# Another instruction order for the engines of a fused attention and two-layer MLP kernel

## The chip, the cores and the metric

The program runs on one core of one Trainium2 chip. The metric is the device time of one execution in microseconds. Three timed runs of the kernel before took 627.49, 627.61 and 626.53 us, a median of 627.49 us. The engines are TensorE (PE in the rows, with PEld for its weight loads), VectorE (DVE), ScalarE (ACT), GpSimd (POOL) and SyncE (SP), whose queue issues nearly all DMAs.

## The reference

```
q_pool = mean of each two neighbouring rows of q          # q, k, v: 2 x 8 heads x 1152 x 64
scores = q_pool @ k^T / 8 ; minus the row's maximum
attn   = exp(scores) / (sum(exp(scores)) + 1e-9)
x      = attn @ v, heads side by side                     # 1152 tokens x 512
x      = g(x @ w_in) @ w_out,  g = h * tanh(softplus(h))  # 512 -> 2048 -> 512
out    = e(x @ w_in2) @ w_out2, e = elu(h)                # 512 -> 2048 -> 512
```

All data is float32.

## The kernel before

The attention works on eight pairs of heads, numbered n = 0 to 7 (batch n // 4). A pair has 576 pooled queries, cut into c = 0 (256) and c = 1 (320), and 1152 keys in nine tiles of 128, numbered kt. Every operand of a score is split into a high and a low part, and three products are added: high with high, low with high, high with low.

The steps of a pair have two-letter names, and the whole attention is one string of such steps, ORDER, which a loop at the end carries out from left to right. Each engine receives its own instructions in that sequence and works them off in that sequence; an instruction whose operands or whose buffer are not ready holds up all that stand behind it on its engine. The names that matter here, each followed by digits for the pair n and then for the piece:

- PM (line 286, also 293, 300, 303) multiplies queries and keys once, for the row maximum alone; PK (line 310, also 312, 314, 318) reduces that product on DVE. TP (lines 324, 327) makes the negated maximum of the pieces.
- FL and FC turn the maximum of pair 0 round through TensorE (line 334) and ACT (lines 341, 345). For the other pairs TO and TI send it through DRAM.
- QK (line 380) is the three products of one tile of scores for c and kt, and a last product (line 387) with "unit" subtracts the maximum. With c = 0 two key tiles are joined in one step. EX (line 398) is the exponential on ACT.
- The sum over the keys has three ways, given for each n and c by a string of nine digits in SUMS, one digit a key tile: 1 adds the tile to a running sum (AD, line 410, on POOL or DVE by its last digit), 2 leaves it to one reduction over neighbouring tiles on DVE (GA, line 415), 0 gives the tile directly to the product with ones on TensorE (SU, line 426). SU also takes the running sum and GA's result: each of these is one source of SU.
- AV (line 471) is the product with v. EV, SP, SO, SI, IN, IO, II, SC, TH, TL bring the sums through DRAM and scale the output.
- LQ, LK, LV load q, k and v; PQ pools q; HQ, DQ (lines 245, 248) and HK, DK (lines 257, 260) split q and k; BQ (line 252) places the last 64 queries. There is one buffer for raw q and one for raw k.
- WR reads a piece of the weights through a ring of three raw buffers. WB (line 119, ACT), WC (line 123, POOL), WS and WW (lines 128, 133, 134, DVE) and WH, WL (lines 142, 145) bring it into its form. A raw buffer is free once WW has read it.

PSUM has four slots of two banks in the attention. The last digit of PM, QK, FL and AV is the slot, so such a step waits until the slot's last reader (PK, EX, FC or EV) is done.

The start of pair 0 stands before ORDER as a few lines of code. The string REST holds the last steps, done between the first units of the MLPs. The MLPs are a fixed sequence of 96 units in bands of 384 tokens, with TensorE products in lines 178 and 709.

Of the kernel before, what the change touches and what calls it, by code (L numbers as in the profile page):

```python
# [22 lines left out]
def tile_pool_attention_mish_elu_mlp(  # L23
# [16 lines left out]
    nc = tc.nc  # L40
# [28 lines left out]
    XH = const.tile([P, KM, NT], F32R, name="XH")  # L69
# [88 lines left out]
    for layer in range(2):  # L158
        c0 = 0
# [23 lines left out]
    def attention():  # L183
        with ExitStack() as st:
# [321 lines left out]
            def ahead_of(i):  # L506
# [26 lines left out]
            LV11 PK07 PQ10 PM083 EX000 PM0c0 PK08 AD0000 AD0030 BQ1 PM091 PK0c HQ1 PM0d2 HK10 PK09 PM0a3 DK100 WB0  # L533
            PK0d PM100 PK0a PM141 QK0062 PK14 WC0 QK0043 EX006 DK110 TP01 PK10 FL11 EX004 DQ10 LK20 PM162 PM120 FC1
            PK16 LQ21 QK0153 LQ20 QK0161 PK12 LK21 EX015 QK0112 EX016 QK0173 AD0051 EX011 QK0130 WS0 EX017 WW0 QK0121
            EX013 PM112 QK0103 EX012 PQ20 PK11 WR30 PM170 EX010 QK0141 WR31 PK17 QK0183 AD0040 EX014 PM132 EX018 PM191
            PK13 PM150 AD0161 AD0130 WH0 QK0083 EX008 TP10 AV00209 PK19 TO10 HQ2 AD0150 HK21 PK15 HK20 TI10 GA00 DK200
            PM263 DK211 EV00 DQ20 PM221 PK26 SU00 LK30 LK31 PM1802 PK22 SP00 WL00 BQ2 SO00 QK1003 PK18 WB1 QK1041 WC1
            SI00 TP11 PM250 TO11 WS1 AV01209 LQ30 WW1 LQ31 TI11 GA01 WH1 WL10 WR40 WB2 PK25 EX100 WC2 IN00 SU01 PQ31
            LV21 EX104 LV20 WS2 EV01 WW2 AD1051 AD1000 QK1110 SP01 BQ3 SO01 PM203 EX111 PM211 IO00 QK1152 PK20 WH2  # L540
            QK1020 EX115 AD1040 PK21 QK1163 EX102 II00 PM242 AD1011 QK1131 EX116 AD1020 PK24 QK1080 SI01 EX113 WR50
            QK1123 EX108 PM231 AD1030 QK1182 EX112 PK23 PM270 EX118 QK1063 WL20 TP20 PK27 TO20 QK1142 EX106 QK1101
            IN01 IO01 PM290 WB3 GA10 AV10309 WC3 WS3 II01 SC00 TH00 EX114 TL00 TI20 WW3 EX110 AD1180 AD1140 SU10 PK29
            PM2823 WR60 WH3 EV10 QK1171 SP10 PK28 SO10 WL30 AV11007 TP21 SC01 TO21 GA11 TH01 HQ3 HK31 DQ30 TI21 EX117
            HK30 TL01 AV11079 DK311 LQ40 LQ41 DK301 PM392 EV11 PM333 PM361 LK41 PK33 SU11 LV30 LK40 PK39 QK2133 SP11
            SO11 PK36 QK2112 EX213 WR41 PM340 EX211 SI10 PM323 PK34 QK2121 PQ40 QK2022 EX212 PK32 PM310 AD2110 AD2120
            QK2041 EX202 PK31 SI11 PM303 QK2002 WR51 EX204 PK30 LV31 PM370 QK2151 AD2041 AD2020 EX200 TP30 QK2183 IN10
            TO30 EX215 IO10 QK2102 AD2011 AD2030 WR61 EX218 QK2161 PK37 EX210 QK2143 EX216 QK2082 AD2101 AD2050 EX214
            PM350 QK2171 IN11 IO11 WB4 GA21 QK2063 EX208 WC4 BQ4 AV20206 EX217 AD2080 EX206 II11 PK35 HK40 AD2060 TI30
            HQ4 DK401 AV20269 II10 HK41 DK411 PM461 DQ41 PM493 LK51 SU20 LK50 PK49 LQ51 PM3802 SP20 LQ50 PK46 SO20  # L550
            AV21309 PK38 TP31 SC10 TO31 SC11 TH10 TH11 TL10 TL11 EV20 TI31 WS4 PQ50 WW4 SU21 EV21 LV40 QK3081 SP21
# [295 lines left out]
```

## Time and profile before

| what | value |
|---|---|
| median of three timed runs | 627.49 us |
| the profiled execution's own time | 623.83 us |
| its span | 621.8 us |
| TensorE busy | 605.3 us, 97% of the span |
| DVE, ACT, POOL busy | 460.5, 338.3, 193.4 us |
| mean granted TensorE clock | 0.992 |
| attention, by the trace | to about 218 us |

The page cuts the span into 40 slices of 15.5 us; the row PEclk is the clock that TensorE was granted in each slice in tenths of full speed, 9 being full (0.9 or more). A busy TensorE is not one at its peak: at half the clock a matmul is busy for twice as long.

### The profile page before, as it was taken

What the parts mean: (1) busy time and instruction counts of PE and PEld (TensorE: products, weight loads), DVE (VectorE), ACT (ScalarE), POOL (GpSimd) and SP (SyncE); (2) the same over time, 40 slices, a digit from 0 to 9 for tenths busy, and PEclk for the clock granted to TensorE, in tenths of its full rate; (3) what the DMA queues carried; (4) which work ended last, traced back from release to release, by engine and by line L of the source; (5) the groups of instructions that cost most, each with busy time, mean ns of one, the idle gap of its engine ahead of it and who ended that gap; (6) DMA issues with size and microseconds to landing.
All of it is one profiled execution on the core that took longest, in us unless ns stands there. A gap on an engine that the chain in (4) does not pass through costs nothing.

```text
span 621.8 us, 11257 instructions
## 1 busy us (share of the span) xinstructions
PE 605.3 (97%) x4434; PEld 534.4 (86%) x4434; DVE 460.5 (74%) x687; ACT 338.3 (54%) x659; POOL 193.4 (31%) x190
## 2 busy tenths in 40 slices
PE   5889999999999999999999999999999999999997
PEld 3757587686786799999999999999999999999996
DVE  5799999899785676754656667669878788995453
ACT  4637485674673464434444453466657666664442
POOL 5665363566965421111132323232210101100000
PEclk9789999999999999999999999999999999999999
DMA  7624243242232035323224222322232123400011
GB/s 213 193 73 122 74 134 106 76 124 70 60 95 57 17 94 164 104 67 101 72 66 135 69 69 67 103 69 70 67 102 69 67 69 106 123 9 17 36 51 51
DMA packets 46958, 53.32 MB, mean 86 GB/s; under 512 B 13818, under 2 KB 36410, under 8 KB 46906
## 3 DMA queue, kind: packets, MB, share of 16 engines
q1 hardware_dynamic: 46762, 52.42, 28.0%
q8 instruction: 34, 0.56, 0.4%
q10 hardware_dynamic: 144, 0.20, 0.1%
q14 instruction: 18, 0.15, 0.1%
HBM read 50.14 MB, written 2.47 MB: 85 GB/s over the span
## 4 chain that ended last, share of the span: by engine, by line
PE 86%; DVE 4%; issue 3%; POOL 3%; ACT 2%; DMA 0%; POOLq 0%; DVEq 0%; ACTq 0%
PE banks L709 32%; PE banks L178 31%; PE banks L471 9%; PE banks L380 7%; PE banks L286 2%; PE banks L387 2%; ACT pt L398 2%; PE banks L426 2%; POOL add L410 1%; DVE stat L310 1%; PE banks L300 1%; DVE wf L133 1%; DVE add L410 1%; PE banks L293 0%; DMA kr<-in_k_dram 0%
## 5 line engine op out<-in xcount | busy, mean ns | idle before, releaser
L178 PE MATMUL banks<-XH,wh 128*128 128x384 f32 x384 | 129.5, 337 | 0.0
L178 PE MATMUL banks<-XL,wh 128*128 128x384 f32 x384 | 129.4, 337 | 0.0
L178 PE MATMUL banks<-XH,wl 128*128 128x384 f32 x384 | 129.4, 337 | 0.0
L123 POOL TENSOR_SCALAR wf<-wf 128x512 f32<-128x512 f32 x64 | 43.3, 678 | 252.2 <-ACT wf L119 214.0
L398 ACT ACTIVATE pt<-banks 128x640 f32<-128x640 f32 (+2 forms) x112 | 82.0, 801 | 17.2 <-PE banks L387 15.4
L310 DVE TENSOR_REDUCE stat<-banks 128x2 f32<-128x1024 f32 (+1 forms) x68 | 77.1, 1167 | 8.8 <-PE banks L286 6.2
L471 PE MATMUL banks<-pt,vr 128*64 128x320 f32 (+1 forms) x576 | 74.1, 411 | 0.8 <-DVE stat L310 0.8
L178 PEld LDWEIGHTS banks<-XH,wh 128*128 128x128 f32 x384 | 72.0, 187 | 2.1 <-issue 0.3
L178 PEld LDWEIGHTS banks<-XL,wh 128*128 128x128 f32 x384 | 72.0, 188 | 1.8
L178 PEld LDWEIGHTS banks<-XH,wl 128*128 128x128 f32 x384 | 72.0, 188 | 0.0
L471 PEld LDWEIGHTS banks<-pt,vr 128*64 128x64 f32 x576 | 40.3, 138 | 30.6 <-issue 2.0
L410 POOL TENSOR_TENSOR add<-add,pt 128x512 f32<-128x512 f32 (+1 forms) x43 | 62.4, 1459 | 8.2 <-DVE add L410 4.3
L709 PE MATMUL banks<-gl,wh 128*128 128x384 f32 x192 | 64.6, 336 | 0.1
L709 PE MATMUL banks<-gh,wl 128*128 128x384 f32 x192 | 64.5, 336 | 0.0
L709 PE MATMUL banks<-gh,wh 128*128 128x384 f32 x192 | 64.4, 335 | 0.0
L663 ACT ACTIVATE gh<-banks 128x384 fp32r<-128x384 f32 x48 | 23.6, 492 | 71.7 <-PE banks L178 71.7
L709 PE MATMUL banks<-wl,gh 128*128 128x512 f32 x144 | 56.2, 390 | 0.0
L709 PE MATMUL banks<-wh,gl 128*128 128x512 f32 x144 | 56.2, 390 | 0.0
L709 PE MATMUL banks<-wh,gh 128*128 128x512 f32 x144 | 56.2, 390 | 0.0
L666 DVE TENSOR_TENSOR gl<-g,gh 128x384 fp32r<-128x384 f32 x48 | 30.6, 640 | 31.1 <-ACT g L664 31.1
L689 ACT CAST gh<-g 128x384 fp32r<-128x384 f32 x48 | 24.7, 514 | 48.1 <-DVE g L683 47.8
L133 DVE SCALAR_TENSOR_TENSOR wf<-raw,wf 128x512 int32<-128x512 int32 x64 | 48.6, 759 | 2.1
(92 smaller groups left out, 1216.5 us busy)
## 6 DMA issues: line engine op xcount, KB each, us to landing
raw<-in_moe_w_in_dram SPq DMA_DIRECT2D x28, 512.0 KB
raw<-in_moe_w_out_dram SPq DMA_DIRECT2D x28, 512.0 KB
vr<-in_v_dram SPq DMA_DIRECT2D x16, 288.0 KB
qr<-in_q_dram SPq DMA_DIRECT2D x14, 288.0 KB
kr<-in_k_dram SPq DMA_DIRECT2D x7, 384.0 KB
out_dram<-part SPq DMA_DIRECT2D x9, 256.0 KB
raw<-in_moe_w_in_dram SPq DMA_DIRECT2D x8, 256.0 KB
raw<-in_moe_w_out_dram SPq DMA_DIRECT2D x8, 256.0 KB
```

Of the source, the lines that this page charges most:

```text
L123: eng.tensor_scalar(self.f, self.f, HUGE, -HUGE, op0=ALU.min, op1=ALU.max)
L133: nc.vector.scalar_tensor_tensor(f, self.top, -0x80000000, f, op0=ALU.bitwise_and, op1=ALU.bitwise_or)
L178: nc.tensor.matmul(pt[:, :TB], w[:, kk * P:(kk + 1) * P], x[:, kk, tk], start=(i == 0), stop=(i == len(terms) - 1))
L310: nc.vector.tensor_reduce(m[:, t, :, j], pt[:, :, :kw], axis=AX.X, op=ALU.max)
L380: nc.tensor.matmul(pt[:, h, t * w:(t + 1) * w], x[half[h], k0:k0 + P], y[half[h], cols], start=(z == t == 0), stop=False,)
L398: nc.scalar.activation(pts[n, c][:, kt:kt + m], pt, AF.Exp, scale=SCALE)
L410: eng.tensor_tensor(d, p[:, ch[0]] if len(ch) == 2 else d, p[:, k], op=ALU.add)
L471: nc.tensor.matmul(acc[n, c][half[h], 0, :w], vs[n][:, h, kt, :], pts[n, c][:, kt, h, :], start=(kt == 0), stop=(kt == KT - 1),)
L663: nc.scalar.activation(gh, h, AF.Mish)
L666: nc.vector.tensor_tensor(gl, g, gh, op=ALU.subtract)
L689: nc.scalar.copy(gh, g)
L709: nc.tensor.matmul(pt, l, r, start=(first and i == 0), stop=(final and i == 2))
```

## The change

The table ORDER is replaced by another sequence of the same steps; the lines of code that began pair 0 become steps of the table (XP, XH, XK, XL, XM); the table SUMS is replaced; one step of REST is exchanged. No other code is touched. In the new SUMS the digits 0 go from 8 to 15 for c = 0 and from 12 to 11 for c = 1, and the strings with at least one 2 go from 4 to 6 for c = 0 and from 8 to 7 for c = 1.

```diff
+                "XP": lambda i, e: pool_q(0, eng[e], (*halves, c1)[i]), "XH": lambda i: high_q(0, (*halves, c1)[i]),
+                "XK": lambda i: high_k(0, ks[i]), "XL": lambda i, e: low_q(0, eng[e], (c0, c1)[i]),
+                "XM": lambda i, e: low_k(0, eng[e], ks[i]),
             }
             SUMS = """
-            100111222 222101100 111111222 022210001 011111101 111022200 111222111 111001222
-            001101101 111111222 111111111 111112221 111111111 111222111 111122111 111122211
+            000111001 000110222 111110000 111010010 000112221 112221111 112221011 110222111
+            101102221 221101101 111222111 111222111 111112221 222111111 111122111 111122111
             """.split()
             ORDER = """
-            WR20 LV00 WR10 PM000 WR11 PM011 PK00 PM022 PK01 PM033 PM040 PK02 PM051 PK03 QA0002 PK04 PK05 QA0023 LK11
-            TP00 LQ10 FL00 LQ11 LK10 PM0b1 WR00 FC0 HK11 WR01 QB002 PK0b PM060 LV10 EX002 LV01 PK06 PM071 WR21 QB000
...
+            WR20 XP01 XH0 LV00 XK0 WR10 XK1 PM000 WR11 XP10 PM011 PK00 XH1 XK2 PM022 XL00 PK01 PM033 XM00 PM040 PK02
+            PM051 XM10 PK03 QA0002 XP20 PK04 XM20 XH2 BQ0 PK05 QA0023 XL10 LK11 TP00 LQ11 FL00 LQ10 LK10 PM061 WR00
...
             REST = [
-                "SP71 SO70",
+                "SP70 SO70",
...
-            pool_q(0, nc.vector, halves[0])
-            high_q(0, halves[0])
-            high_k(0, ks[0])
...
-            blk_q(0)
-            low_q(0, nc.gpsimd, c1)
```

Three places show what moves. The first is TensorE's queue from the turning of pair 0's maxima (line 334) on. KH_117 and KH_121 are pair 0's keys, KH_198 those of pair 1. Before:

```order
L334 MATMUL banks_74<-ident_97,pad_95 128x128 x2
...
L303 MATMUL banks_74<-KH_117,blk0_87 128x384
L286 MATMUL banks_74<-KH_117,QH_114 128x384 x2
L286 MATMUL banks_74<-KH_198,QH_234 128x512 x2
L293 MATMUL banks_74<-KH_198,QH_234 128x128 x8
L380 MATMUL banks_74<-QH_114,KH_117 128x256 x2
```

With the change:

```order
L303 MATMUL banks_74<-KH_121,blk0_87 128x384 x2
L286 MATMUL banks_74<-KH_121,QH_116 128x384 x2
L380 MATMUL banks_74<-QH_116,KH_121 128x256 x2
...
L387 MATMUL banks_74<-top0_83,unit_91 128x512 x2
L286 MATMUL banks_74<-KH_198,QH_235 128x512 x2
L334 MATMUL banks_74<-ident_97,pad_95 128x128 x3
L286 MATMUL banks_74<-KH_198,QH_235 128x512 x2
L293 MATMUL banks_74<-KH_198,QH_235 128x128 x8
L380 MATMUL banks_74<-QH_116,KH_121 128x320 x2
```

A step of scores of pair 0 now stands ahead of the first product of pair 1, the turning of the second maxima stands right behind that product, and the scores with c = 1 (320 wide) follow at once.

The second place is DVE's queue behind the maxima of pair 0 (stat_139, stat_127). stat_246 and stat_257 belong to pair 1, stat_466 and stat_465 to pair 2. Before:

```order
L312 TENSOR_REDUCE stat_246<-banks_74 128x2x4
L324 TENSOR_REDUCE pad_95<-stat_139 128x4
L327 TENSOR_REDUCE pad_95<-stat_139 128x2
L310 TENSOR_REDUCE stat_246<-banks_74 128x2 x3
L410 TENSOR_TENSOR add_227<-add_227,pt_209 128x512
L128 TENSOR_SCALAR wf_243<-wf_243 128x512
L133 SCALAR_TENSOR_TENSOR wf_243<-raw_195,wf_243 128x512
L134 SCALAR_TENSOR_TENSOR wf_243<-raw_195,wf_243 128x512
L310 TENSOR_REDUCE stat_246<-banks_74 128x2 x3
L324 TENSOR_REDUCE neg_247<-stat_246 128x2x2
L310 TENSOR_REDUCE stat_246<-banks_74 128x2 x2
L415 TENSOR_REDUCE add_227<-pt_209 128x512
```

With the change:

```order
L324 TENSOR_REDUCE pad_95<-stat_127 128x4
L327 TENSOR_REDUCE pad_95<-stat_127 128x2
L310 TENSOR_REDUCE stat_257<-banks_74 128x2 x2
L312 TENSOR_REDUCE stat_257<-banks_74 128x2x4
L128 TENSOR_SCALAR wf_254<-wf_254 128x512
L133 SCALAR_TENSOR_TENSOR wf_254<-raw_195,wf_254 128x512
L134 SCALAR_TENSOR_TENSOR wf_254<-raw_195,wf_254 128x512
L310 TENSOR_REDUCE stat_257<-banks_74 128x2 x4
L324 TENSOR_REDUCE neg_258<-stat_257 128x2x2
L310 TENSOR_REDUCE stat_257<-banks_74 128x2 x2
L260 TENSOR_TENSOR KL_455<-kr_306,KH_454 128x768
L248 TENSOR_TENSOR QL_450<-qr_292,QH_449 128x576
```

Pair 0's last maximum (lines 324, 327) goes ahead of the wide reduction of line 312, the weights' words (lines 128 to 134) move up by two peaks, the add and the reduction of line 415 leave this stretch, and two lower parts of pair 2 come to DVE.

The third place is SP's queue at the loads of pair 2 (qr_309, kr_299 before; qr_292, kr_306 now). Before:

```order
L236 DMA vr_207<-in_v_dram 128x576
L224 DMA kr_299<-in_k_dram 128x768
L230 DMA qr_309<-in_q_dram 128x576 x2
L224 DMA kr_299<-in_k_dram 128x384
L109 DMA raw_385<-in_moe_w_out_dram 128x512 x2
```

With the change:

```order
L230 DMA qr_292<-in_q_dram 128x576 x2
L224 DMA kr_306<-in_k_dram 128x384
L109 DMA raw_359<-in_moe_w_out_dram 128x512 x2
L224 DMA kr_306<-in_k_dram 128x768
L236 DMA vr_384<-in_v_dram 128x576
```

The wide load of pair 2's keys and the load of pair 1's v now stand behind a weight load that waits for a raw buffer.

## Rows read from the trace of the kernel before

**Rows 1.** The page: busy time of the engines, and the granted clock in 40 slices.
```profile
PE 605.3 (97%) x4434; PEld 534.4 (86%) x4434; DVE 460.5 (74%) x687; ACT 338.3 (54%) x659; POOL 193.4 (31%) x190
...
PEclk9789999999999999999999999999999999999999
```

**Rows 2.** Windows: from:to, length, busy us (instructions) by engine, granted clock, DMA share, GB/s.
```profile
10.80:17.75 6.95, 4.66 (x25) 2.34 (x23) 5.40 (x8) 3.22 (x7) 2.67 (x3) 0.98 0.83 254
17.75:24.70 6.95, 5.50 (x42) 4.87 (x43) 3.90 (x7) 3.50 (x5) 5.42 (x5) 0.53 0.62 199
24.70:34.30 9.60, 7.96 (x89) 6.62 (x87) 8.50 (x8) 7.61 (x14) 5.34 (x4) 1.00 0.35 110
34.30:38.00 3.70, 3.32 (x20) 2.24 (x20) 3.67 (x5) 1.43 (x3) 1.27 (x1) 0.54 0.30 102
38.00:60.00 22.00, 21.51 (x265) 15.63 (x265) 20.49 (x24) 12.16 (x24) 12.90 (x10) 1.00 0.39 110
60.00:218.00 158.00, 156.69 (x1820) 116.78 (x1817) 132.15 (x169) 94.10 (x163) 91.54 (x68) 1.00 0.30 81
```

**Rows 3.** Waits of TensorE: who waited for whom, us in total, times, longest.
```profile
PE banks L286 <- DVE stat L310: 4.8, 4, 2.5
...
PE banks L471 <- DVE stat L310: 0.8, 1, 0.8
```

**Rows 4.** Timeline, 14 to 25 us: start, length, engine, line, operation, idle before and releaser.
```profile
15.79 1.40 POOL L240 TENSOR_TENSOR qr<-qr 128x576 f32<-128x576 f32 x1 [4.28 <-DMA qr<-in_q_dram]
...
17.23 0.50 ACT L252 CAST blk<-qr 64x64 fp32r<-64x64 f32 x2 [1.78 <-POOL qr L240]
...
18.32 0.83 ACT L257 CAST KH<-kr 128x768 fp32r<-128x768 f32 x1
19.20 0.80 PE L286 MATMUL banks<-KH,QH 64*128 64x512 f32 x2 [2.50 <-DVE stat L310]
...
20.54 0.52 PE L380 MATMUL banks<-QH,KH 64*128 64x256 f32 x2
...
22.35 0.41 PE L380 MATMUL banks<-QH,KH 64*128 64x256 f32 x2
```

**Rows 5.** Timeline, 24 to 40 us, all engines.
```profile
26.49 6.35 ACT L398 ACTIVATE pt<-banks 128x640 f32<-128x640 f32 x9 [0.57 <-PE banks L387]
...
29.06 1.80 DVE L133 SCALAR_TENSOR_TENSOR wf<-raw,wf 128x512 int32<-128x512 int32 x1
30.90 1.66 DVE L134 SCALAR_TENSOR_TENSOR wf<-raw,wf 128x512 int32<-128x512 int32 x1
...
36.45 4.84 PE L471 MATMUL banks<-pt,vr 128*64 128x256 f32 x36
```

**Rows 6.** Timeline, 40 to 53 us, TensorE.
```profile
41.90 0.65 PE L426 MATMUL banks<-pt,ones 128*32 128x128 f32 x16
...
42.91 0.79 PE L300 MATMUL banks<-KH,blk 128*128 128x512 f32 x3
43.63 0.39 PE L380 MATMUL banks<-QH,KH 64*128 64x256 f32 x2
...
44.67 0.29 PE L380 MATMUL banks<-QH,KH 64*128 64x256 f32 x2
...
45.95 5.07 PE L471 MATMUL banks<-pt,vr 128*64 128x320 f32 x36
50.94 1.02 PE L426 MATMUL banks<-pt,ones 128*32 128x160 f32 x24
...
52.44 0.42 PE L380 MATMUL banks<-QH,KH 64*128 64x320 f32 x2
```

**Rows 7.** Groups of DVE by line and shape: busy us, mean ns, idle before.
```profile
L310 DVE TENSOR_REDUCE stat<-banks 128x2 f32<-128x1024 f32 x56 | 66.2, 1214 | 5.7 <-PE banks L286 3.1 <-ACT top L345 2.5
L133 DVE SCALAR_TENSOR_TENSOR wf<-raw,wf 128x512 int32<-128x512 int32 x64 | 48.6, 759 | 2.1
...
L410 DVE TENSOR_TENSOR add<-add,pt 128x512 f32<-128x512 f32 x8 | 6.8, 852 | 3.7 <-POOL add L410 3.7
...
L260 DVE TENSOR_TENSOR KL<-kr,KH 128x768 fp32r<-128x768 f32 x4 | 4.2, 1054 | 0.6 <-ACT KH L257 0.6
```

More of the change, by code (lines that the diff above doesn't have):

```diff
@@ L535, in attention @@
[L535 to L539, printed above, removed]
@@ new lines, in attention @@
+            WH2 QK1040 EX110 SI01 WL20 EX111 PM291 WR50 QK1173 WR51 EX104 PK29 QK1062 AD1010 WB3 QK1160 EX117 WC3
+            AV10106 EX106 WS3 IN01 WW3 IO01 AD1140 AD1171 WH3 AV10169 EX116 SC00 WL30 II01 TH00 TL00 PM203 AD1040
+            QK1182 WR60 PK20 EV10 WR61 PM270 EX118 SU10 AD1100 PK27 PM2821 SP10 SO10 QK1133 PQ30 WR40 PK28 PM210 WR41
+            EX113 SC01 QK1121 PK21 TH01 BQ3 AV11302 EX112 TP20 TP21 HQ3 TO20 TL01 AV11329 TO21 AD1111 HK31 DQ30 HK30
+            DK301 TI20 AD1120 TI21 PM392 EV11 PM360 SI10 PM331 PK39 DK310 LQ41 SU11 LK41 PK36 LV31 QK2042 SP11 LK40
@@ new lines, in attention @@
+            PK33 SO11 PM350 LV30 QK2023 EX204 PK35 PM371 QK2112 EX202 PK37 QK2180 EX211 QK2123 AD2041 AD2030 IN10
+            EX218 IO10 PM341 QK2172 EX212 PK34 AD2180 AD2110 QK2080 SI11 EX217 LQ40 QK2133 EX208 PM321 AD2171 QK2102
+            EX213 AD2080 QK2140 PK32 EX210 QK2153 EX214 QK2162 IN11 AD2100 EX215 IO11 GA21 QK2001 EX216 PM300 PQ40
+            PM313 EX200 QK2062 II11 AD2161 WB4 AV20106 AD2150 BQ4 EX206 PK30 II10 HK40 PK31 WC4 HQ4 AV20169 DK400 HK41
+            TP30 GA20 TO30 PM462 PM490 DK410 SU20 PK49 TI30 DQ40 PM3831 LK51 SP20 PK46 LK50 AV21009 LQ50 PK38 SO20
@@ new lines, in attention @@
+            TP31 WS4 TO31 WW4 LQ51 SC10 WH4 SC11 TI31 TH10 TH11 TL10 SU21 TL11 EV20 PM422 EV21 PQ50 SI20 QK3083 SP21
+            PK42 LV41 PM441 EX308 SO21 QK3040 WL40 PK44 PM433 QK3062 EX304 PK43 PM451 QK3100 AD3080 AD3050 EX306 PK45
+            QK3183 EX310 SI21 QK3132 AD3070 IN20 EX318 IO20 PM401 QK3120 LV40 EX313 PK40 WR70 AD3181 AD3100 QK3173
+            EX312 QK3162 EX317 II20 QK3140 EX316 AD3171 QK3111 EX314 AD3160 PM473 IN21 QK3002 IO21 EX311 PK47 PM410
+            QK3021 EX300 AD3110 PK41 QK3153 EX302 II21 TP40 AV30209 AD3010 EX315 GA30 TO40 HQ5 AD3000 HK51 BQ5 GA31
@@ new lines, in attention @@
+            AD5070 EX508 AD5121 AD5171 PM623 QK5140 EX516 QK5041 AD5110 EX514 IN41 PK62 IO41 QK5022 EX504 PM650 TP60
+            GA51 QK5103 AD5080 EX502 AV50109 BQ7 II41 AD5020 GA50 TO60 AD5160 PK65 SU50 SC40 TI60 PM6821 TH40 EX510
+            QK5180 TL40 PK68 EV50 AD5100 AV51308 SP50 SO50 TP61 SC41 TO61 WR71 TH41 SI50 EX518 TL41 TI61 HK70 AD5180
+            HK71 HQ7 AV51389 DQ71 PM711 EV51 LV71 DK711 PM792 LV70 SU51 PK71 QK6000 SP51 WB7 SO51 PK79 PM731 QK6043
+            EX600 PK73 PM722 QK6020 EX604 PK72 SI51 PM741 WE0 AD6040 AD6010 EX602 QK6173 PK74 QK6142 EX617 QK6160
@@ new lines, in attention @@
+            AD6000 IN51 EX614 IN50 IO51 PM701 IO50 QK6083 EX616 PK70 QK6122 AD6020 EX608 QK6100 EX612 TP70 PM773
+            QK6151 EX610 AD6030 PK77 QK6182 EX615 QK6110 II50 AD6161 AD6140 EX618 QK6131 EX611 QK6063 TO70 EX613 GA61
+            AD6080 PM762 PM750 EX606 AV60109 AD6150 GA60 TI70 AD6180 II51 PK76 AD6130 SU60 PK75 PM7831 SP60 SO60
+            AD6170 AV61209 PK78 SI60 DK700 TP71 TO71 IN60 SC51 TI71 TH51 TL51 SC50 SU61 EV61 IO60 TH50 QK7000 TL50
+            EV60 SP61 QK7023 EX700 QK7061 EX702 AD7000 AD7010 II60 QK7132 EX706 QK7140 SO61 QK7113 EX713 AD7060 QK7121
```

75 lines of the change are left out of this document (23 added, 52 removed).

## The prediction

> **What bounds the kernel now.** I read the page first [rows 1]: TensorE is busy for 605.3 of 621.8 us, so no other engine can give much by itself; what can be won is TensorE's idle time and its slow time. The clock row says where the slow time is: the second and third slices, 15.5 to 46.5 us, are below full, and from there on every slice is full. So I cut that stretch finer [rows 2]. From 17.75 to 24.70 us the granted clock is 0.53, and from 34.30 to 38.00 us 0.54, which is the 1.2 GHz level; between and after them it is 1.00, which is 2.4 GHz. In the same rows TensorE's idle time is the length less the busy time: 2.29, 1.45, 1.64, 0.38 and 0.49 us, then 1.31 us over the 158 us to the end of the attention. Third, the waits [rows 3]: TensorE's maximum products (line 286) waited 4.8 us for DVE in four waits, the longest line. Before both clock drops TensorE stood idle, 2.50 us until 19.20 [rows 4] and 1.64 us in the window that ends at 34.30 [rows 2].
>
> The whole prize follows. Idle from 10.8 to 38 us is 5.76 us. The slow stretches hold 5.50 and 3.32 us of busy time, of which full clock would give back 5.50 x 0.47 = 2.6 and 3.32 x 0.46 = 1.5 us. With the 1.8 us of idle behind 38 us that is 11.7 us at most. The MLPs have nothing to give, as their instructions and their order are the same.
>
> But TensorE is not alone in that stretch. DVE is busy 8.50 of 9.60, 3.67 of 3.70 and 20.49 of 22.00 us [rows 2], so from 24.7 to 60 us TensorE can only run ahead if DVE does. DVE's own idle time lies before: 3.05 us between 17.75 and 24.70.
>
> **The change part by part.**
>
> *The start of pair 0* as steps of the table: the queues begin with the same instructions in the same sequence. Nothing up to 10.8 us. The exchanged step in REST is one of two small copies beside TensorE's units: nothing, and if it were late the first unit that needs those tokens lies over ten units on.
>
> *From 10.8 to 19.2 us.* DVE has eight peaks of pair 0 to do, either way, and pair 1's first product still hangs on the chain of q: its DMA lands at 15.79, POOL pools it for 1.40, ACT does three casts from 17.23 to 18.32 + 0.83 = 19.15 [rows 4]. The change swaps two of the casts, which leaves the end of the chain. So TensorE begins pair 1 at 19.2 as before. What is new is that one step of scores stands ahead of it. It costs 1.81 us at the low clock (20.54 to 22.35) [rows 4] and 1.04 at the full one (43.63 to 44.67) [rows 6], and its slot comes free when the sixth of the eight peaks is done, about 16.1. It fits into the old wait of 2.50 us. Pair 0's last maximum is no longer queued behind line 312's reduction of pair 1 on DVE, so the turning of the maxima, the casts behind it and the first of the nine tiles with c = 1 come at about 22 us instead of 25.7.
>
> *From 20 us, DVE's queue* to the third peak of pair 2, which frees the slot for AV of c = 1: twelve peaks of the big form at 1.17 (mean 1.21 less the overlap of neighbours) [rows 7] make 14.0; the weights' words, one short and two of 0.76 [rows 7], 2.1; the two parts of K at 1.05 or less [rows 7] and one of Q between them, 2.5; small ones 0.3. That is 18.9, so 38.9 us. Words cost 1.80 and 1.66 [rows 5] where POOL worked beside them; there POOL waits for pair 2's q by my placing, so I take 0.76, and 2.0 us more is the other bound. TensorE's own chain to this point: nine tiles at ACT's pace, 6.35 us in all [rows 5], from 22.3 to 29; the other two joined steps, the first AV at 30.4 and 4 us long, three peaks' products, sums, the side product and one step of scores, ending at 38.9 too. The first AV then starts at 30.4 instead of 36.45 [rows 5], the second at 38.9 instead of 45.95 [rows 6]. In the run before one more step of scores (0.95 to 1.04) lay ahead of that second AV, so the lead is 7.05 - 1.0 = 6.0 us, if the clock stays full from 10.8 on.
>
> *The clock.* The gap that is left, from 17.5 to 19.2, is 1.7 us instead of 2.5, with more work ahead of it; whether the clock falls again I can't read from the rows. The bounds are 0 and the 2.6 us above; I take half, 1.3. The second drop's cause, the wait at 32 to 33.7, is gone in my placing, as the next gap is under 1 us. Lead 4.7 us.
>
> *The sums.* Sources of SU rise from 20 to 29 for c = 0 (seven more digits 0, two more strings with a reduction) and fall from 28 to 26 for c = 1. One costs (42.91 - 41.90) / 4 = 0.25 us, or (52.44 - 50.94) / 5 = 0.30 us with c = 1 [rows 6]: 9 x 0.25 - 2 x 0.30 = +1.65 us on TensorE, which nothing hides. Two of them lie before the second AV and are in the placing above: +1.15 remains.
>
> *What DVE gains.* Adds of the 512 form go from 8 to 1, 7 x 0.85 = 6.0 us [rows 7]; three more adds of the 640 form at about the same take 2.6 back. Six more tiles in reductions of c = 0 and five fewer of c = 1 cancel nearly, and among the splits of q and k, two poolings and three parts of K leave and two parts of Q and one of the weights come, another 1 to 2 us off. Some 5 us less over the attention, off the path except where TensorE waited for DVE: of the 1.8 us of idle behind 38 us I take half, 0.9. The bounds are the whole 1.8 and, as the new sequence may make new waits, a loss of the same size.
>
> *SP.* The wide load of pair 2's keys and v of pair 1 now stand behind a weight load that waits for the words on DVE. By the placing these end at 25.4, so the keys are issued at about 26 and are wanted by ACT only at 32. Nothing, with 3 us to spare.
>
> Sum: 4.7 - 1.15 + 0.9 = 4.45 us less. Against the profile's own 623.83 us (span 621.8) that makes 619.4. That execution is 3.66 us below the median of the runs, which lie at 626.5 to 627.6; the same gain from the median is **623.0 us**.
>
> One rule of the Trainium skill speaks against this change, in "TensorE: Matmul & The Clock Gate", section "What's actually happening": where the rise comes varies from run to run of the same kernel, and one shouldn't fit a plan to one count of slow matmuls. The trace before can't show it, being one execution; only that all three timed runs lie above it. By that rule the clock's share of the gain would come in some runs only, and the time would be that of the next case.
>
> **The rivals.**
>
> *The clock falls at both places again.* For: DVE still sets the pace of pair 0's peaks, which leaves TensorE thin from 12 to 17 us, and a gap of 1.7 us stays. Against: more work ahead of the gap and no long gap behind. The lead of 6.0 loses 2.6 and 1.5 and is 1.9; less 1.15 for the sums, with the later waits as they were, 0.75 us is won: 626.7 us.
>
> *Everything comes.* No drop at all and no later waits: 11.7 - 1.65 leaves 10.0 us at most; with the old chain of q still there, the lead of 6.0 - 1.15 + 1.8 = 6.65. So 617.5 to 620.8, say 620.
>
> *Slower: the weight load on SP.* If the words on DVE wait for their raw piece, DVE's peaks stand behind them in the queue and pair 2's keys stand behind the next weight load on SP. Before, the words ended at 30.90 + 1.66 = 32.56 [rows 5]. Were they as late here, the keys would be issued at 33.5 instead of 26, ACT's casts, wanted at 32, would come at about 39, and pair 2's first products, placed at 34.5, at about 40: 5.5 to 6 us lost, and DVE 7 us late with its peaks. From a word's end of about 29 us on the lead is eaten; at 32.6 the time is 627.5 - 4.45 + 6 = 629. For: the queues hold it so. Against: the piece's loads are issued as early as before, and POOL's part stands behind one split of K only.
>
> *The change doesn't do what it says* is the first rival; that TensorE's order is really different the rows of the order show.
>
> **How the numbers follow.** My forecast 0.50, with its own range of 621 to 625.5; the first rival 0.18; everything comes 0.17; slower 0.15. The range of 617.5 to 628.5 leaves out half of the slower case and a little at the lower end. Two tenths of a per cent, 1.25 us, is about what runs of this kernel can tell from no change. Faster takes the forecast, the good case and a little of the first rival, in all 0.69; same takes most of that rival, 0.16; slower 0.15.
>
> **What would show it.** Right: a first AV near 30.4 us and a second near 39, DVE without its idle 3 us between 17.75 and 24.7, no second clock drop, the product with ones 1.65 us longer in sum. Half wrong: a clock of 0.5 from about 18 to 25 with the same lead of DVE. Wrong: a first AV after 35 us, words on DVE that end after 29, or new waits of TensorE above 2 us in total between 60 and 218.

## The result, and the profile after

The changed kernel took 618.86 us, the median of four runs (618.01 to 619.40), against 627.01 (626.52 to 627.61) for four runs of the kernel before beside it. The ratio is 0.9868, with an interval of 0.9851 to 0.9885. The gain is 8.15 us. The forecast of 623.0 lies 4.0 us below this comparison's 627.01, and the sum behind it gave 4.45: the direction was right and the size too small by almost half.

The profiled execution took 618.69 us by its own time, with a span of 616.9 and a mean clock of 0.996; the one before had 623.83, 621.8 and 0.992. Profile against profile the gain is therefore 5.14 us, close to the 4.45 of the sum. So two questions are open: what the order did, and why the medians lie further apart than the profiles.

The page of the changed kernel, to be read against [rows 1]: busy time and share of each engine, and the granted clock in 40 slices.

```profile
PE 604.1 (98%) x4490; PEld 534.4 (87%) x4490; DVE 450.7 (73%) x682; ACT 338.7 (55%) x659; POOL 190.8 (31%) x189
...
PEclk9899999999999999999999999999999999999999
```

TensorE is busy for 1.2 us less although it runs 56 instructions more, and only one slice is still below full clock. Windows of the changed kernel over almost the same stretches as [rows 2]: length, busy us (instructions) of PE, PEld, DVE, ACT and POOL, granted clock, DMA share, GB/s.

```profile
10.80:17.75 6.95, 6.05 (x41) 3.31 (x37) 5.62 (x8) 3.25 (x6) 3.11 (x3) 1.00 0.81 257
17.75:24.70 6.95, 5.30 (x42) 4.94 (x44) 6.08 (x9) 5.12 (x10) 3.78 (x3) 0.76 0.35 101
24.70:34.30 9.60, 9.31 (x108) 7.56 (x106) 7.70 (x8) 8.11 (x14) 6.72 (x5) 0.99 0.55 188
34.30:38.00 3.70, 3.70 (x64) 2.48 (x64) 3.60 (x6) 0.58 (x2) 0.00 (x0) 1.00 0.12 9
38.00:60.00 22.00, 21.79 (x269) 15.71 (x259) 16.84 (x24) 13.12 (x22) 11.60 (x11) 1.00 0.41 128
60.00:213.00 153.00, 152.06 (x1803) 113.86 (x1802) 123.86 (x159) 92.42 (x161) 92.03 (x67) 1.00 0.32 82
```

The second clock drop is gone: 34.30 to 38.00 us stands at 1.00 and TensorE is busy without a gap. The first drop is still there, but half as long: between 21.4 and 24.6 us the clock is 0.50, the 1.2 GHz level, which is why the second row has 0.76 and not 0.53. DVE is busy for 6.08 us in that row instead of 3.90. Behind 38 us TensorE's idle time is 0.21 + 0.94 = 1.15 us instead of 1.80. The waits of TensorE up to the end of the attention (us in total, times, longest), to be read against [rows 3]:

```profile
PE banks L286 <- ACT KH L257: 4.8, 2, 4.7
PE banks L286 <- ACT QH L245: 1.7, 1, 1.7
PE banks L286 <- DVE stat L310: 0.8, 2, 0.5
```

The wait of line 286 for DVE's peaks fell from 4.8 us in four waits to 0.8 in two. The long one for ACT's keys is the wait for the first loads, ahead of 10.8 us. The second line is the new wait ahead of pair 1, and it ends on a cast of q. TensorE's timeline (start, length, engine, line, operation, idle before and what ended it), against [rows 4 to 6]:

```profile
17.27 0.39 PE L387 MATMUL banks<-top,unit 64*128 64x512 f32 x2
19.40 0.50 PE L286 MATMUL banks<-KH,QH 64*128 64x512 f32 x2 [1.74 <-ACT QH L245]
...
21.48 0.58 PE L380 MATMUL banks<-QH,KH 64*128 64x320 f32 x2
...
32.03 4.11 PE L471 MATMUL banks<-pt,vr 128*64 128x256 f32 x36
...
40.27 5.07 PE L471 MATMUL banks<-pt,vr 128*64 128x320 f32 x36
```

The gap ahead of pair 1 is 1.74 us (placed: 1.7). The scores with c = 1 begin at 21.48 instead of about 25.7, the first AV at 32.03 (placed: 30.4), the second at 40.27 (placed: 38.9). Against the 45.95 of before the second AV leads by 5.68, less 1.0 for the step of scores that no longer stands ahead of it: 4.7, as forecast. DVE's words and SP's loads in the same trace:

```profile
24.70 0.69 DVE L134 SCALAR_TENSOR_TENSOR wf<-raw,wf 128x512 int32<-128x512 int32 x1
...
26.31 0.43 SPq L224 DMA_DIRECT2D kr<-in_k_dram  x1
```

The words take 0.69 us, not the 1.66 to 1.80 that they took beside POOL [rows 5], and end at 25.4 as placed; the keys of pair 2 are issued at 26.3 (placed: about 26). The products with ones, before and then with the change, over the whole span (length, PE busy, PEld busy, clock, DMA share, GB/s):

```profile
0.00:618.00 618.00, 15.09 (x384) 10.40 (x384) 0.99 0.28 85
```

```profile
0.00:618.00 618.00, 16.71 (x440) 11.78 (x440) 1.00 0.29 86
```

They grew by 1.62 us (forecast: 1.65).

### The profile page after: what moved, and what is told of

It reads as the page before. It is cut to its first block, busy times and chain, and to the rows that moved or that the text cites. A ratio compares the mean times of both kernels' runs of the same rounds, so it can differ in the third digit from the quotient of the medians.

```text
span 616.9 us, 11358 instructions
## 1 busy us (share of the span) xinstructions
PE 604.1 (98%) x4490; PEld 534.4 (87%) x4490; DVE 450.7 (73%) x682; ACT 338.7 (55%) x659; POOL 190.8 (31%) x189
## 4 chain that ended last, share of the span: by engine, by line
PE 88%; POOL 3%; DVE 3%; issue 2%; ACT 2%; DMA 2%; SPq 0%; POOLq 0%; DVEq 0%; ACTq 0%
PE banks L178 33%; PE banks L698 32%; PE banks L471 9%; PE banks L380 7%; PE banks L387 2%; PE banks L286 2%; PE banks L426 2%; POOL add L410 1%; PE banks L300 1%; ACT pt L398 1%; DMA qr<-in_q_dram 1%; DMA pop<-tot 1%; DVE stat L310 1%; POOL qr L240 0%; PE banks L293 0%
## 5 line engine op out<-in xcount | busy, mean ns | idle before, releaser
L398 ACT ACTIVATE pt<-banks 128x640 f32<-128x640 f32 (+2 forms) x112 | 82.3, 793 | 12.0 <-PE banks L387 10.8
L410 POOL TENSOR_TENSOR add<-add,pt 128x512 f32<-128x512 f32 (+1 forms) x40 | 57.9, 1457 | 10.3 <-ACT pt L398 7.4
L128 DVE TENSOR_SCALAR wf<-wf 128x512 int32<-128x512 int32 x64 | 38.2, 596 | 14.2 <-POOL wf L123 14.2
```

Source lines behind the costliest of these rows:

```text
L128: nc.vector.tensor_scalar(f, f, 3, None, op0=ALU.logical_shift_left)
L398: nc.scalar.activation(pts[n, c][:, kt:kt + m], pt, AF.Exp, scale=SCALE)
L410: eng.tensor_tensor(d, p[:, ch[0]] if len(ch) == 2 else d, p[:, k], op=ALU.add)
```

## The experiments

The theory to begin with: most of the surplus is the clock. The kernel before loses more to it than its one profile shows, and it loses differently from run to run. The rivals: the order itself is worth more than forecast, through the early maximum or through the adds taken off DVE and POOL. The runs lie on four chips, each kernel beside runs of the kernel before on the same chip; the kernel before has medians of 624.71 to 625.22 us on the four, so times can also be set side by side across them, to about half a microsecond. The chip of the first comparison is not on record. A run's mean granted clock stands beside its time where it matters. In kernels with a new kind of step the lines behind it have numbers 13 or 14 higher, and one higher in the copies that have only a comment added.

**The kernel before, again.** One comment line is added.

> The kernel before, unchanged, to see the clock and span of each run and a second profile. Open: its timed runs lie at 626.5 to 627.6 us but its profiled execution at 623.83 (mean clock 0.992), while the changed kernel's four executions lie at 618.0 to 619.4. Theory A (clock): the usual executions have some 3 us more of TensorE's work at the low clock than the profiled one, so their mean clock is near 0.985 or below, and a profile in the usual state shows one slow stretch more or a longer one before 60 us. Rival B (waits): the mean clock is 0.992 in all of them and the 3 us lie in a wait, such as a DMA that lands later.

> The kernel before, one look, for a profile in the usual state. In 50 runs its clock was 0.986 to 0.997 and its time 620.98 to 629.14 us, while its two profiles were at 0.992 (623.83) and 0.994 (624.05). Theory A: an execution at 0.989 or below shows a slow stretch of 3 to 4 us more than the two of the first profile, or longer ones, before 60 us, and is 2 to 3 us longer for it. Rival B: the same stretches, and the time in waits elsewhere.

> As the look before it, for a third profile of the kernel before: theory A a slow stretch that is placed or as long as its clock says, 0.001 of the mean clock being 1.2 us at the low level; rival B none of it.

Measured: 624.85 us (623.05 to 627.57), ratio 1.0 (0.9979 to 1.0022); two further single executions took 623.53 (clock 0.992) and 626.33 (0.989). The slower one has a longer slow stretch, as theory A had it, but a longer wait as well. The clock's behaviour in this kernel is not one thing. Windows of the first copy and then of the third:

```profile
17.50:24.00 6.50, 4.69 (x38) 4.29 (x38) 4.24 (x7) 3.33 (x6) 5.70 (x5) 0.52 0.61 197
...
34.00:37.50 3.50, 3.34 (x36) 2.23 (x36) 3.46 (x5) 2.30 (x4) 1.98 (x3) 1.00 0.09 21
37.50:41.00 3.50, 3.50 (x52) 2.23 (x49) 3.50 (x3) 0.37 (x1) 3.50 (x3) 1.00 0.04 1
```

```profile
17.50:24.00 6.50, 4.93 (x38) 4.37 (x38) 4.25 (x7) 3.09 (x5) 5.53 (x5) 0.51 0.64 198
...
34.00:37.50 3.50, 2.63 (x14) 1.76 (x14) 3.46 (x5) 0.33 (x1) 1.07 (x1) 0.52 0.42 150
37.50:41.00 3.50, 3.50 (x18) 1.95 (x18) 3.50 (x3) 2.30 (x4) 0.93 (x1) 0.51 0.08 6
```

The first drop is in every profile of this kernel. The second is missing in one, 3.5 us long in two [rows 2], and 6.8 us long in another; in that one the 36 products of the first AV take 5.75 us instead of 4.11. Over 50 timed runs on two chips the same program lay between 620.98 and 629.14 us, at clocks of 0.986 to 0.997: the 20 runs at 0.989 or less have a median of 626.6, the 10 at 0.996 or more one of 622.8. The clock is not all of the scatter: those 20 runs alone lie between 624.44 and 629.14 us.

What comes ahead of the second drop differs from run to run too, and it lies on DVE and POOL. The timelines of the kernel before, of the first copy and of the third: POOL's pooling of pair 2's q, the weights' words on DVE, and TensorE's wait for the peak behind them.

```profile
28.88 1.43 POOL L240 TENSOR_TENSOR qr<-qr 128x576 f32<-128x576 f32 x1 [4.91 <-DMA qr<-in_q_dram]
...
33.74 0.75 PE L286 MATMUL banks<-KH,QH 64*128 64x512 f32 x4 [1.64 <-DVE stat L310]
```

```profile
28.86 0.69 DVE L134 SCALAR_TENSOR_TENSOR wf<-raw,wf 128x512 int32<-128x512 int32 x1
29.13 1.71 POOL L241 TENSOR_TENSOR qr<-qr 128x576 f32<-128x576 f32 x1 [5.04 <-DMA qr<-in_q_dram]
29.59 1.81 DVE L135 SCALAR_TENSOR_TENSOR wf<-raw,wf 128x512 int32<-128x512 int32 x1
...
32.58 0.74 PE L287 MATMUL banks<-KH,QH 64*128 64x512 f32 x4 [0.69 <-DVE stat L311]
```

```profile
28.26 1.49 POOL L241 TENSOR_TENSOR qr<-qr 128x576 f32<-128x576 f32 x1 [4.43 <-DMA qr<-in_q_dram]
28.37 1.67 DVE L129 TENSOR_SCALAR wf<-wf 128x512 int32<-128x512 int32 x1
...
31.77 1.91 DVE L135 SCALAR_TENSOR_TENSOR wf<-raw,wf 128x512 int32<-128x512 int32 x1
...
34.87 1.93 PE L287 MATMUL banks<-KH,QH 64*128 64x512 f32 x6 [3.01 <-DVE stat L311]
```

The three operations on the words take 0.42, 0.69 and 0.69 us when they begin before POOL does, and 1.66 to 1.91 us each when they begin while POOL works. In the first copy one of the three falls beside POOL's work, in the kernel before two [rows 5], in the third copy all three. TensorE's wait behind them is 0.69, 1.64 and 3.01 us, and the slow stretch that follows 0, 3.5 and 6.8 us. The second copy fits, with two of the three, 1.68 us and 3.5 us. In the whole profile of the kernel before, each of these operations that took over 1 us began while POOL worked. This is read from profiles; no run moves POOL's work alone.

The drops don't add up simply, though. The first copy had no second drop and took 624.05, the profile with both took 623.83. The first copy's second AV came at 44.60 instead of 45.95 us, but its third at 62.11 instead of 62.29: what TensorE wins there, the old order loses again to DVE, for whose peak TensorE waits 1.69 us until 55.66 in this copy and 0.49 us until 55.83 in the kernel before.

**The kernel before with the first wait filled.** A new step repeats the matmuls of a maximum product, with nothing changed in the result; 18 matmuls run in the 2.5 us wait ahead of pair 1. The second kernel also repeats a tile of scores ahead of the second drop; the third is the first once more, on another chip.

```
+def again(n, e, r):                  # the step RP
+    t, j = evs(n)[e]
+    for _ in range(r):
+        for h in range(2):
+            nc.tensor.matmul(sc[n, e][:, h, :KB], rows(n, h, t), ..., start=True, stop=True)
-... PK09 PM0a3 DK100 WB0
+... PK09 PM0a3 RP0a9 DK100 WB0
-... QK0183 AD0040                    (before_fill12 only)
+... QK0183 RQ0182 AD0040
```

> The kernel before with TensorE's wait before pair 1's first product (16.7 to 19.2 us) filled: the last maximum product of pair 0 is repeated nine times, 18 matmuls that only write the same values again. Nothing else moves. Theory A: the clock doesn't fall at 17.75, the stretch to 24.7 runs at 2.4 GHz, and up to 2.6 us are won, 624 to 625 us. Rival B (DVE sets the pace in that stretch): the clock may stay, but DVE's peaks come no earlier, and the time is 626.5 to 627.6 as before.

> As the kernel before with the first wait filled, and the second wait (32.1 to 33.7 us) filled too by doing the ninth tile of scores with c = 1 three times. Theory A: no clock drop at all behind 11 us, 4 us less than the kernel before, 622.5 to 624. Rival B: 626.5 to 627.6, or up to 1 us more, since the repeats delay one exponential by 1.2 us.

> The kernel before with its first wait filled, once more, as the base of the next two on one chip: 619 to 620.6 us at a clock of 1.000 if the clock is what the filling works through; a time and clock like those of the kernel before if the first result was chance.

Measured: 620.11 us (618.75 to 622.05), ratio 0.9919 (0.9897 to 0.9942); with the tile repeated as well 621.27, ratio 0.9937 (0.9916 to 0.9958), so the second filling adds nothing; again 620.77 (617.63 to 622.17), ratio 0.994 (0.9918 to 0.9963). All three lie well below the 624 to 625 and 622.5 to 624 us that were expected of the first two. Of the 17 runs with the one filling, 11 have a clock of 0.999 or more, with medians of 619.99 and 619.47. In the profile of the first kernel, one of the other six (622.05 us, 0.997), the clock stays full through both places and falls only at about 53 us. Windows of the third kernel, and then its timeline:

```profile
17.75:24.70 6.95, 5.72 (x69) 4.88 (x66) 4.91 (x8) 5.00 (x11) 5.88 (x5) 1.00 0.54 180
...
34.30:38.00 3.70, 3.70 (x55) 2.33 (x52) 3.70 (x4) 0.37 (x1) 3.70 (x3) 1.00 0.04 1
```

```profile
16.63 1.73 PE L310 MATMUL banks<-KH,QH 64*128 64x384 f32 x18
...
19.58 0.51 PE L287 MATMUL banks<-KH,QH 64*128 64x512 f32 x2 [1.23 <-ACT KH L258]
...
32.06 4.11 PE L485 MATMUL banks<-pt,vr 128*64 128x256 f32 x36 [0.15 <-DVE stat L324]
...
41.16 5.07 PE L485 MATMUL banks<-pt,vr 128*64 128x320 f32 x36
```

Useless work of 1.73 us keeps the clock at 1.00 through both places, and in the old order the two AVs come 4.4 and 4.8 us earlier than in [rows 5, 6]. That shows the price of the low clock in the kernel before, together with all that it sets off: 624.94 - 619.99 = 4.95 us on one chip, 624.71 - 619.47 = 5.24 on another. One thing that it sets off is the late words. Here they come some 2 us earlier and end before POOL begins, as in all profiles with this filling:

```profile
27.92 0.69 DVE L135 SCALAR_TENSOR_TENSOR wf<-raw,wf 128x512 int32<-128x512 int32 x1
29.27 1.43 POOL L241 TENSOR_TENSOR qr<-qr 128x576 f32<-128x576 f32 x1 [4.66 <-DMA qr<-in_q_dram]
```

**The changed kernel again, and filled.** In the first filled kernel the early step of scores is repeated twice; in the second it is repeated once, and some of pair 0's maximum products as well.

```
-... PK0c QK0041 DK100 WB0 ...
+... PK0c QK0041 RQ0042 DK100 WB0 ...                 (after_fill)
+... PM070 RP073 ... PM0b1 RP0b1 ... PM0a1 RP0a1 ... PM082 RP083 ... PM093 RP093 ... QK0041 RQ0041 DK100   (after_fill2)
```

> The changed kernel, unchanged, beside runs of the kernel before on one chip, to see its clock and span run by run. In the job before this one the kernel before ran at 622.3 (mean clock 0.997) to 628.6 us (0.986), and with its first wait filled at 618.75 to 620.6 (1.000). Theory A (the new order removes most of the low clock as well as waits): the changed kernel's runs lie at 0.994 to 0.997, 618 to 619.5, with a spread under 2 us against 6 us of the kernel before. Rival B (the clock had nothing to do with the change's gain): its clock and spread are those of the kernel before, 0.986 to 0.997.

> The changed kernel with its remaining wait (17.5 to 19.4 us) filled: its early step of scores is done three times, 1.7 us more work in the wait. In the changed kernel the clock was 0.50 from about 21.4 to 24.6 us. Theory A: that drop goes too, and 1 to 1.6 us are won: 617.3 to 617.9 us. Rival B: the peaks of DVE and the exponentials set the pace there: 618.5 to 619 as before.

> The changed kernel with its wait filled by one repeat of the early step of scores, and with eleven repeated pairs of maximum products of pair 0 in the thin stretch from 12 to 17 us as well, where the profiles of the filled and of the changed kernel on this chip show the clock fall at 16 us. Theory A: every run has a clock of 1.000 and lies at 616.2 to 616.7 us, about 2 us below the changed kernel's median of 618.4. Rival B (the repeats hold up DVE's peaks, which set the pace): 617 us or more at a clock of 1.000.

Measured: unchanged 618.36 us (616.23 to 619.08), ratio 0.9882 (0.984 to 0.9925); filled 616.39 (616.23 to 619.15), ratio 0.9866 (0.9842 to 0.9891); filled further 616.92 (616.64 to 617.38), ratio 0.9864 (0.9839 to 0.9889). The unchanged kernel's clocks of 0.996 to 1.000 speak for theory A, though its spread is 2.85 us and not under 2. The first filling brought more than theory A had (616.39 against 617.3 to 617.9), with four of six runs at 1.000; in its profile, one of the other two, the clock falls at 16 us all the same. The second lies between its two theories. The unchanged one's single run at clock 1.000 took 616.23, as much as the first filled kernel's at that clock (616.23 to 616.43). So a half drop goes with about 2.0 us in the median of the changed kernel. In the unchanged one's new profile the drop lies at another place:

```profile
12.00:14.00 2.00, 1.32 (x8) 0.59 (x9) 1.13 (x2) 0.88 (x2) 0.33 (x1) 1.00 0.73 215
14.00:16.00 2.00, 1.81 (x11) 0.85 (x11) 2.00 (x3) 1.36 (x2) 1.00 (x2) 1.00 0.99 368
16.00:19.50 3.50, 3.50 (x24) 2.68 (x20) 3.43 (x5) 2.58 (x5) 2.04 (x2) 0.51 0.93 293
```

Here the clock fell ahead of pair 1, behind idle time of no more than 0.68 and 0.19 us in two rows, and the wait for pair 1 is hidden in the slow stretch: the second AV begins at 38.98 us, as in the second filled kernel, and this execution took 617.30. What a half drop costs depends on where it falls. The filled kernels have the lowest medians of all that ran, but their intervals overlap that of the changed kernel. What the second surely has is steadiness: four runs within 0.74 us, at 0.999 to 1.000.

**The early step of scores moved back.** It stands ahead of the new wait; here it stands behind the product that ends the wait.

```
-... HQ1 PK0c QK0041 DK100 WB0 PK09 PM102 EX004 ...
+... HQ1 PK0c DK100 WB0 PK09 PM102 QK0041 EX004 ...
```

> The changed kernel with one step moved back: the early step of scores (QK0041 with its exponential) stands behind pair 1's first product again, so that TensorE waits from about 16.5 to 19.4 us. Theory A: the clock falls before 19 us in most runs and stays low for 4 to 7 us, mean clock 0.988 to 0.994; with the step itself 1 us later that is 621 to 623 us. Rival B: only the step's own 0.9 us is lost, at a clock of 0.994 to 0.997: 619.5 to 620 us.

Measured: 619.82 us (619.04 to 622.08), ratio 0.9921 (0.9891 to 0.9951), at clocks of 0.991 to 0.994; some 1.5 us more than the changed kernel on that chip. The clock is that of theory A, the time that of rival B. Its profile's window:

```profile
16.50:23.50 7.00, 6.23 (x30) 4.53 (x30) 4.91 (x7) 4.39 (x9) 3.93 (x4) 0.51 0.38 113
```

The whole first drop is back, and none of the ten runs reaches the 0.996 that each run of the changed kernel on that chip has. This one step makes the difference between a half drop and a whole one.

**The second maximum late again.** In the filled changed kernel the turning of pair 0's second maxima goes back behind DVE's wide reduction of pair 1.

```
-... EX004 TP01 WC0 PK10 FL10 DQ10 PM133 FC1 PM141 PK13 QK0162 ... PK14 ...
+... EX004 WC0 PK10 DQ10 PM133 PM141 PK13 PK14 TP01 FL10 FC1 QK0162 ...
```

> The changed kernel with its wait filled (616.4 us at clock 1.000), and with pair 0's last maximum (TP01) behind the wide reduction of pair 1 on DVE again, with the turning of the maxima behind it, as in the kernel before. Theory A (the lead of DVE is a part of its own): the scores with c = 1 come about 3 us later, TensorE waits 2 to 3 us at 21 to 25 us, and 2 to 3 us are lost even where the clock stays: 618.4 to 619.5, more where it falls. Rival B (order on DVE counts for nothing once the clock is full): under 0.7 us lost, 616.4 to 617.1.

Measured: 623.05 us (620.87 to 625.09), ratio 0.9958 (0.993 to 0.9985): theory A, and more than it had. A wait for the turned maxima stands in the profile, behind it DVE's last word falls beside POOL's pooling (1.95 us from 26.72 on, against 0.69 in the filled kernel), and then the clock is low:

```profile
25.61 0.94 PE L347 MATMUL banks<-ident,pad 128*128 128x128 f32 x6 [2.08 <-DVE pad L337]
```

```profile
27.00:30.50 3.50, 3.50 (x29) 3.39 (x27) 1.67 (x1) 2.03 (x5) 2.81 (x2) 0.51 0.18 57
```

At a clock of 0.996 to 0.997 these runs take 620.87 to 621.71, the filled kernel's two at that clock 618.36 and 619.15: about 2.4 us at a like clock, and the rest of the 6.7 between the medians goes with lower clocks (0.989 to 0.995 in the other eight runs).

**The early maximum alone.** The same step, put early in the filled kernel before.

```
-... RP0a9 ... PM100 PK0a PM141 QK0062 PK14 WC0 QK0043 EX006 DK110 TP01 PK10 FL11 EX004 DQ10 LK20 PM162 PM120 FC1
+... RP0a9 ... PM100 PK0a TP01 FL11 QK0062 FC1 PK10 PM141 PK14 WC0 QK0043 EX006 DK110 EX004 DQ10 LK20 PM162 PM120
```

> The same base with pair 0's last maximum ahead of pair 1's wide reduction on DVE, its turning on TensorE and ACT right behind pair 1's first product, and one step of scores between; the scores of c = 1 keep their places. Theory A (that place on DVE holds most of the 3.7 us that the new order wins at full clock): 1.5 to 3 us faster than its base, 617 to 618.5. Rival B (the words of the weights and the peaks behind set the pace anyway): within 0.7 us of its base.

Measured: 621.43 us (619.97 to 623.08), ratio 0.9961 (0.9938 to 0.9983). At full clock its median is 620.55, 1.1 us above the 619.47 of the filled kernel without the edit, whose runs at that clock lie between 617.63 and 620.77. Theory A, that this edit carries the gain of the order, fell. In the new order the step is needed where it is; alone, in the old one, it gives nothing.

**The direct tiles.** First eight of the direct tiles of c = 0 are given back to adds in the filled changed kernel, the adds placed by hand; then seven are made direct in the filled kernel before.

```
-SUMS 000111001 ... 111110000 ... 000112221 ...      (after_fill_sums)
+SUMS 111111011 ... 111111100 ... 110112221 ...      with AD0000 AD0010 ... AD2000 AD2011 added
-SUMS 100111222 ... 111111222 ... 011111101 ...      (before_fill1_sums)
+SUMS 100100222 ... 000111222 ... 001101101 ...      with AD0051 AD0040 AD1000 ... AD2041 removed
```

> The changed kernel with its wait filled (616.4 us), and eight of its direct key tiles (c = 0 of pairs 0 to 2) given back to running sums: four adds on DVE, four on POOL, eight sources of 8 matmul records fewer on TensorE, at 0.25 us each 2.0 us. Theory A (the direct tiles are a price that TensorE pays in full and their relief of DVE and POOL is worth less): 614.5 to 615.8 us. Rival B (they pay for themselves, as TensorE would wait for the adds): 616.4 us or more.

> The same with seven key tiles of c = 0 (two of pair 0, three of pair 1, two of pair 2) made direct: their adds, three on DVE and four on POOL, are taken out of the order and nothing is moved. Theory A (a net price, as predicted: 7 x 0.25 = 1.75 us on TensorE, some of it back where TensorE waited for DVE): 0.5 to 1.75 us slower than its base, 620.5 to 621.8 us. Rival B (the adds held TensorE up more than that, as the 16 us lost with eight tiles given back would have it): 1 us or more faster than its base, under 619 us.

Measured: giving back took 634.36 us (632.54 to 636.76), ratio 1.0144 (1.0098 to 1.0189), 18 us above the filled kernel, so rival B came; making direct took 619.73 (619.51 to 620.41), ratio 0.993 (0.9907 to 0.9953), which lies in neither theory's range. Where the 18 us go, the first kernel's timeline shows at the first of these adds:

```profile
32.33 3.99 POOL L423 TENSOR_TENSOR add<-add,pt 128x512 f32<-128x512 f32 x3
...
36.35 1.49 DVE L423 TENSOR_TENSOR add<-add,pt 128x512 f32<-128x512 f32 x2 [1.91 <-POOL add L423]
```

DVE stands for 1.91 us until POOL has finished its adds, its peaks stand behind, and TensorE waits for those; the second AV comes at 45.17 instead of 40.53 us and the clock falls at four places. As I chose the places of the adds, this gives the direction but not the size. The other one is the cleaner test: its seven tiles were expected to cost TensorE 1.75 us, and its products with ones did grow by 1.5 (16.61 us over the whole span, from 15.09), but at a clock of 0.999 or more its median is 619.72 against 619.47, a difference well inside the base's scatter at that clock. What TensorE pays here it gets back, as nearly as these runs can tell, from the engines that are relieved. Its eight runs lie within 0.9 us. The test is one of the old order; in the new one no such test was clean.

## Why the prediction was right or wrong

**Right: the placing.** The gap ahead of pair 1, the end of the words, SP's order, the missing second drop, the price of the sums and the lead of 4.7 us at the second AV all came as the prediction worked them out. The first AV was 1.6 us late and the second 1.4; in the profile of the second filled kernel, where the clock stays at 1.00 from 10.8 us on, they begin at 30.73 and 38.98, within 0.4 us of the 30.4 and 38.9 that were placed for a full clock:

```profile
30.73 4.11 PE L484 MATMUL banks<-pt,vr 128*64 128x256 f32 x36
...
38.98 5.07 PE L484 MATMUL banks<-pt,vr 128*64 128x320 f32 x36
```

That the clock cost the second AV 40.27 - 38.98 = 1.3 us, as forecast, is luck: the 1.3 was half of a bound, taken without a row.

**The clock's term: right in size, not in what makes it up.** It was put at 4.1 us in the kernel before and 1.3 left in the changed one, a gain of 2.8. The filled kernels give 4.95 and 5.24 before and about 2.0 after, a gain of 3.0 to 3.2. But the 4.1 was summed from TensorE's slow time alone. The 4.95 and 5.24 also hold the words, 1.80 and 1.66 us beside POOL against 0.69 twice, ahead of the peak that TensorE waits for. The prediction noted their price and did not see that it is the first slow stretch that pushes them beside POOL, nor that the number that falls there changes from run to run.

**The first step that failed: "the same gain from the median".** The sum was made against one execution at a clock of 0.992, which took 623.83 us, and then taken off a median of 627.49 as if both kernels scattered alike. They don't: the kernel before lies anywhere in 620.98 to 629.14 us, the changed one in 616.23 to 619.40. The prediction itself noted that its profile lay 3.66 us below the median and drew nothing from it. On the chip of the second comparison the gain of the medians is 624.98 - 618.36 = 6.62 us; the first gave 8.15, with the kernel before at 626.5 to 627.6. On the four chips of the experiments 10 of 83 executions lie in that band, nine of them at a clock of 0.989. But four out of four is more than that scatter would give, and neither the clock of these runs nor their chip was recorded: what makes the last 1.5 us stays open.

**The second, mis-sized: the order at full clock.** 6.0 - 4.1 - 1.15 + 0.9 = 1.65 us was forecast. With the clock full on both sides the kernels differ by 619.99 - 616.35 = 3.6 us on one chip, or by 619.47 - 616.35 = 3.1 across two; against the second filled kernel's 616.92 it is 3.1 and 2.6. One part is the term of the sums, +1.15 us, priced as one "which nothing hides": the test of the direct tiles, in the old order, gave 0.25 us net, no more than noise, where 1.75 was summed. The relief of DVE and the price on TensorE belong together, and I counted the first at half, 0.9 us. Windows behind 38 us of the filled kernel before (the third) and of the second filled changed kernel:

```profile
38.00:60.00 22.00, 21.21 (x247) 15.86 (x248) 20.92 (x27) 12.84 (x23) 12.21 (x11) 1.00 0.40 113
60.00:208.00 148.00, 146.69 (x1710) 109.50 (x1708) 124.66 (x157) 89.80 (x154) 89.39 (x65) 1.00 0.31 85
```

```profile
38.00:60.00 22.00, 21.81 (x267) 15.83 (x271) 16.68 (x24) 13.81 (x24) 12.91 (x12) 1.00 0.37 111
60.00:208.00 148.00, 147.50 (x1748) 110.55 (x1739) 119.86 (x154) 90.26 (x156) 90.73 (x67) 1.00 0.32 83
```

TensorE's idle time there goes from 2.10 to 0.69 us, 1.4 us instead of the 0.9. The rest isn't settled. Between these two profiles 1.3 us are won by the first AV (32.06 to 30.73), and 1.95 by the start of the MLPs (211.75 to 209.80). The early maximum alone does not make them; which of the moves together do stays open.

So of the 3.7 us that the forecast was short, by the first filled kernel's numbers, 1.5 to 2.0 are the order at full clock, 0.2 to 0.4 the clock's term, and about 1.5 the high times of the kernel before in the first comparison. The theory that the experiments began with, that most of the surplus is the clock, is not borne out: the rival, the order itself, carries about half.

**The rivals.** The first, a fall of the clock at both places, came in no profile of the changed kernel. The slower one, words late on DVE, did not come: they end at 25.4. "Everything comes" was worked out as 617.5 to 620.8, and that is where the median lies, but not by its way, since a half drop stayed. The rule of the Trainium skill ("TensorE: Matmul & The Clock Gate", "What's actually happening"), that the place of the rise varies from run to run, agrees with the changed kernel, whose slow stretch lay at 21.4 to 24.6 us in one profile and at 16.0 to about 19.5 in the next. The second slow stretch of the kernel before, 0, 3.5 or 6.8 us long, is no case of it, since the wait ahead of it differs as well (0.69 to 3.01 us). I used the rule against the changed kernel, but the runs of the unchanged one spread more, over 8.2 us against 3.2 (83 and 10 executions).

## What to carry to other kernels

Where the granted clock of a profile is below full anywhere, don't take one execution's gain off a median: run the kernel many times, read the clock of each run, and size the clock's term by a version whose waits are filled. Where runs of one program scatter, also compare the durations of the same instruction between profiles, and what ran beside it, before the clock is given all the blame. A short wait early in a kernel can be worth filling, with real work if some can be moved there and with repeated matmuls if not. Work moved from an engine that holds TensorE's slots to TensorE itself should be priced with what that engine's relief gives back.

## What the runs showed of the hardware

The clock fell behind stretches in which TensorE was never idle for long: 2.50 us in [rows 4], 1.74 us in the changed kernel, and in another profile of that kernel 0.68 and 0.19 us within the 4 us ahead of the fall. 18 matmuls (1.73 us) in a wait of 2.5 us were enough to keep it in 11 of 17 runs, and moving one step of scores by one place in TensorE's queue turned a drop from 3.2 to 7 us. One program without any change had mean clocks of 0.986 to 0.997; the medians of its runs at 0.989 or less and at 0.996 or more lie 3.8 us apart.

Between 23 and 34 us the same DVE operation on 128x512 words (lines 133 and 134 of the kernel before) took 0.69 us when it began before POOL's work and 1.66 to 1.95 us when it began during it; for the short operation ahead of it these were 0.42 and 1.67 us.
